# The projections' stores whose data ScalarE makes, moved from SyncE's DMA queue to ScalarE's

## The chip, the core and the metric

The kernel runs on one core of a Trainium2 chip. A core has TensorE (PE, matmuls into PSUM banks), VectorE (DVE), ScalarE (ACT), GpSimd (POOL) and SyncE (SP), which here only issues DMAs. Each engine works through its own instructions in order. A DMA is an instruction on the queue of the engine that issues it; the 16 DMA engines carry it out. The metric is the device time of one execution, in microseconds (us), lower is better. Before the change the median of three runs is 1646.94 us (1646.8 to 1649.85).

## What is computed

Two attentions over the same shapes (2048 positions, width 576, 32 heads of 18) stand side by side in the output. A is local: each position looks at 8 earlier positions, two apart. B is a full softmax attention. Both begin with a projection and end with another.

```python
def _A_ref(x, wqkv, wo):
    qkv = (lambda x, *d: x.transpose(*d))((x @ wqkv).reshape(B, S, 3, H, Dh), 2, 0, 3, 1, 4)
    ...
    logits = jnp.where(mask[None, None, :, :], logits, -1e9)
    attn = _softmax(logits, axis=-1)
    o = jnp.einsum("bhsw,bhswd->bhsd", attn, vg)
    return (lambda x, *d: x.transpose(*d))(o, 0, 2, 1, 3).reshape(B, S, D) @ wo

def _B_ref(x, wqkv, wo):
    ...
    scores = jnp.einsum("bhqd,bhkd->bhqk", q, k) * scale
    p = _softmax(scores, axis=-1)
    o = jnp.einsum("bhqk,bhkd->bhqd", p, v)
    return (lambda x, *d: x.transpose(*d))(o, 0, 2, 1, 3).reshape(B, S, D) @ wo

return jnp.concatenate([a, b], axis=-1)
```

## The kernel before

**Stages.** The projections of both attentions come first (0 to about 423 us), then the main stage: B's scores, exponentials and weighted sums step by step, with A's local attention on GpSimd beside it, and the output projections at the end. The change lies in the projections.

**How a projection is made.** Inputs and weights are split into a high and a low part, so that three products of the short format give the long one's accuracy. A loaded chunk (tiles `first`, `raw`, `more`) is rounded by ScalarE into the high part (`xhi`, `whi`, `ahi`; L369), and DVE or GpSimd subtracts to get the low part (`xlo`, `wlo`, `alo`; L370). The fifth, half-sized chunk goes through `xhl` and `whh` (L369, L404 to L406). TensorE multiplies the parts into a PSUM bank.

**How B's results leave** (`leave`, L456). For each third of the columns, each block of 512 positions and each of three row chunks, ScalarE copies the bank to `olo` (L461, which frees the bank), rounds that to `ohi` (L462), and GpSimd subtracts one from the other (L463). Then both go to the DRAM tensor `dqk` (L468): one store each for chunks 0 and 2 (128 rows), two each for chunk 1 (64 rows each, as its rows belong to queries and keys). That is 36 results with 48 stores of `ohi` and 48 of `olo`. `ohi` and `olo` have four buffers each, so the fifth result waits until the first one's store has landed. Later loads bring `dqk` back as the stacked operands `qs` and `ks` (L143, L144, on GpSimd's queue).

**How A's results leave** (`leave_a`, L649). ScalarE copies the bank to an `ohi` buffer (L651), and one store takes it to `da` (L652): 56 results, 56 stores.

**The first part (to about 83 us)** makes one third of B's queries and keys, then half of the values. The order of ScalarE's work is written out by hand: a list `ahead` of splits is popped between the chunks of the product, and the results of the block before leave in between (L503 to L519). So between 34 and 46 us ScalarE alternates: a result leaves, then a split of the next block's input or of the value weights (`whi` at L369), which the first value products need.

**The stream (83 to about 423 us)** (`stream`, L286) takes the products in groups of four over four steps; in each step two products run on the two halves of TensorE's rows. Four banks hold the group. Two products end with the third step and two with the fourth, and the next group takes their banks one step later. Between the matmuls stand the maxima of B's scores (`take` and `reduce`, L156 to L166): a matmul and a maximum on DVE. After each step `slot` runs what is due: loads of inputs (L363), of A's weights (L418, L423), splits, and loads on GpSimd's queue. When all maxima of a block are there, `mh` and `mt` (L104, L105) are loaded into two rows of `qs`, with eight small loads on SyncE's queue (L192). The last group has the first exponentials `e` (L235) in it.

**Queues.** `load` is `nc.sync.dma_start`: nearly all loads and stores stand on SyncE's queue, in the order of the program. Four first loads stand on ScalarE's, and the stacked operands' first loads on GpSimd's. The framework gives each DMA of SyncE's and ScalarE's queues one of eight semaphores in turn, and has it wait for the landing of the DMA that used the same semaphore before.

Of the kernel before, what the change touches and what calls it, by code (L numbers as in the profile page):

```python
# [7 lines left out]
F32 = mybir.dt.float32  # L8
# [23 lines left out]
HALO = DIL * (W - 1)  # L32
# [27 lines left out]
def two_attentions(ctx: ExitStack, tc, xa, wa, woa, xb, wb, wob, out):  # L60
# [5 lines left out]
    nc = tc.nc  # L66
    load = nc.sync.dma_start
# [19 lines left out]
    dqk = dram.tile([2, 2 * D, S], F32, name="dqk")  # L87
# [3 lines left out]
    da = dram.tile([3 * D, HALO + S], F32, name="da")  # L91
# [247 lines left out]
    with (tc.tile_pool(name="x", bufs=1, side="right") as xp,  # L339
# [104 lines left out]
        if True:  # L444
# [11 lines left out]
            def leave(i, b, c, ps):  # L456

                hi = xp.tile([128, 512], F32R, name="ohi", bufs=4)
                lo = low.tile([128, 512], F32R, name="olo", bufs=4)
                whole = lo.bitcast(F32)  # L460
                nc.scalar.activation(whole, ps, AF.Copy)  # L461
                nc.scalar.activation(hi, whole, AF.Copy)  # L462
                nc.gpsimd.tensor_sub(lo, whole, hi)  # L463
                for k, t in enumerate((hi, lo)):
                    at = 0
                    for base, c0, n in chunks[c]:
                        first = base + third * i + c0
                        load(dqk[k, first : first + n, 512 * b : 512 * b + 512], t.bitcast(F32)[at : at + n])  # L468
                        at += n


# [31 lines left out]
            for b in range(NB):  # L503
                pss = [bank() for _ in range(3)]
                for c in range(5):
                    for k, ps in enumerate(pss):
                        partly(c, ps, w0, x[b], slice(128 * k, 128 * k + 128), every)
                    for _ in range(2 if b == 0 and c < 3 else 1):
                        if ahead:
                            ahead.popleft()()  # L510
                    if c > 1 and out_of:
                        leave(*out_of.pop(0))
                out_of = [(0, b, k, ps) for k, ps in enumerate(pss)]
                if b == 2:
                    for c in range(5):
                        vw[1][1](c)
            do_all(ahead)
            for o in out_of:
                leave(*o)  # L519
# [120 lines left out]
            for k in range(2, 14):  # L640
                n = 46 if k == 2 else 36 + 4 * k
# [7 lines left out]
            def leave_a(c, b, n, ps):  # L649
                o = xp.tile([128, 512], F32, name="ohi", bufs=4)  # L650
                nc.scalar.activation(o[:n], ps, AF.Copy)  # L651
                load(da[128 * c : 128 * c + n, HALO + 512 * b : HALO + 512 * b + 512], o[:n])  # L652


            order = [t for i in (0, 8) for j in range(4) for t in (i + j, i + j + 4)]
# [11 lines left out]
            for b0 in range(0, NB, 2):  # L667
                for i, w in ((1, w1), (2, w2)):
                    for c in range(3):
                        for b in (b0, b0 + 1):  # L670
                            work_list.append(((b % 2, w, xs[b], slice(128 * c, 128 * c + 128), every),
                                              lambda ps: ps, lambda ps, i=i, b=b, c=c: leave(i, b, c, ps)))
# [3 lines left out]
            for c, b in order:  # L676
                n = min(128, 3 * D - 128 * c)
                work_list.append(((b % 2, ws[c][0], xas[b][0], slice(0, n), every),
                                  lambda ps, n=n: ps[:n], lambda ps, c=c, b=b, n=n: leave_a(c, b, n, ps)))
# [442 lines left out]
    while step < ALL:  # L1122
        n, kt = divmod(step, NT)
        g, b = divmod(n, NB)
# [46 lines left out]
```

## Time and profile before

| | |
|---|---|
| median of three runs | 1646.94 us (1646.8 to 1649.85) |
| the profiled execution | 1648.65 us, its span 1646.9 us |
| granted TensorE clock, mean | 1.0 |
| instructions | 33732 |
| DMA | 188.22 MB in 188353 packets, mean 114 GB/s |

How to read the profile: *busy* is the time in which an engine carries out an instruction; issuing a DMA is not busy. SPq and ACTq are the queues of SyncE and ScalarE: their rows give the start of an issue, its length, and the DMA. `out<-in` names the tiles, `L468` is a line of the kernel, `x2` the number of instructions in a row. In brackets behind a row stands the idle time of the engine before it and what ended it. The chain of work is followed back from the last instruction, at each step to what released it; a DMA in it is counted from its issue to its landing. Matmuls overlap, so their durations do not add up; their starts tell the pace.

The page's DMA view of the whole run, for orientation (a tenth of the busy share of the 16 DMA engines for each of 40 equal slices; the projections are the first ten):

```profile
DMA  8937955422616346157238225616525132034201
```

### The profile page before, as it was taken

What the parts mean: (1) busy time and instruction counts of PE and PEld (TensorE: products, weight loads), DVE (VectorE), ACT (ScalarE), POOL (GpSimd) and SP (SyncE); (2) the same over time, 40 slices, a digit from 0 to 9 for tenths busy, and PEclk for the clock granted to TensorE, in tenths of its full rate; (3) what the DMA queues carried; (4) which work ended last, traced back from release to release, by engine and by line L of the source; (5) the groups of instructions that cost most, each with busy time, mean ns of one, the idle gap of its engine ahead of it and who ended that gap; (6) DMA issues with size and microseconds to landing.
All of it is one profiled execution on the core that took longest, in us unless ns stands there. A gap on an engine that the chain in (4) does not pass through costs nothing.

```text
span 1646.9 us, 33732 instructions
## 1 busy us (share of the span) xinstructions
PE 1635.5 (99%) x12906; PEld 938.5 (57%) x12906; DVE 1395.2 (85%) x2386; ACT 1222.5 (74%) x2419; POOL 960.6 (58%) x800
## 2 busy tenths in 40 slices
PE   9999999999999999999999999999999999999999
PEld 7999778999433444444344344344444344344676
DVE  5199999999899989889889889899899999898533
ACT  6424432111899998998998998998998998998544
POOL 2406642210095995994994994994995997920000
PEclk9999999999999999999999999999999999999999
DMA  8937955422616346157238225616525132034201
GB/s 235 250 116 204 256 166 139 133 89 90 95 43 105 96 135 123 68 130 137 67 90 155 88 70 143 128 64 123 132 79 117 66 107 78 21 114 136 88 37 59
DMA packets 188353, 188.22 MB, mean 114 GB/s; under 512 B 118384, under 2 KB 132208, under 8 KB 186464
## 3 DMA queue, kind: packets, MB, share of 16 engines
q1 hardware_dynamic: 183328, 174.53, 40.9%
q0 software_dynamic: 4032, 10.63, 3.1%
q8 instruction: 101, 1.65, 0.4%
q10 hardware_dynamic: 832, 0.92, 0.2%
q14 instruction: 60, 0.49, 0.1%
HBM read 113.16 MB, written 88.12 MB: 122 GB/s over the span
## 4 chain that ended last, share of the span: by engine, by line
PE 93%; DMA 4%; ACT 1%; DVE 1%; POOL 0%; issue 0%; SPq 0%; ACTq 0%; POOLq 0%
PE po L700 30%; PE bank L229 25%; PE bank L322 14%; PE bank L159 13%; PE bank L1001 7%; PE bank L259 3%; DMA den<-o 1%; DMA dqk<-olo 1%; DMA dqk<-ohi 1%; DMA first<-wb 1%; DMA raw<-xa 1%; POOL xlo L370 0%; DMA raw<-xb 0%; DMA first<-xb 0%; PE bank L976 0%
## 5 line engine op out<-in xcount | busy, mean ns | idle before, releaser
L166 DVE TENSOR_REDUCE mx<-bank 128x1 f32<-128x512 f32 x2048 | 1286.9, 683 | 145.1 <-PE bank L159 113.7
L235 ACT ACTIVATE e<-bank 128x512 f32<-128x512 f32 x2048 | 1060.2, 613 | 95.0 <-PE bank L229 57.4
L159 PE MATMUL bank<-ks,qs 54*128 54x512 f32 x2048 | 751.0, 423 | 2.5 <-DVE mx L166 2.4
L229 PEld LDWEIGHTS bank<-qs,ks 56*128 56x128 f32 x2048 | 330.0, 185 | 450.2 <-ACT e L235 424.6
L229 PE MATMUL bank<-qs,ks 56*128 56x512 f32 x2048 | 581.5, 425 | 0.0
L700 PE MATMUL po<-e,v 128*19 128x512 f32 x4096 | 539.6, 599 | 0.0
L159 PEld LDWEIGHTS bank<-ks,qs 54*128 54x128 f32 x2048 | 340.6, 184 | 15.8 <-DVE mx L166 8.8
L832 POOL TENSOR_TENSOR pr<-aq,akv 128x1024 f32<-128x1024 f32 x72 | 158.4, 2200 | 28.3 <-DMA akv<-dpart 25.8
L700 PEld LDWEIGHTS po<-e,v 128*19 128x19 f32 x4096 | 69.5, 96 | 179.7 <-issue 169.3
L875 POOL TENSOR_TENSOR pr<-lg,akv 128x1024 f32<-128x1024 f32 x72 | 158.1, 2196 | 0.6
L836 POOL TENSOR_TENSOR pr<-pr 128x1024 f32<-128x1024 f32 x64 | 152.4, 2381 | 5.0
L651 ACT ACTIVATE ohi<-bank 128x512 f32<-128x512 f32 (+1 forms) x56 | 30.5, 595 | 147.3 <-issue 115.7
L322 PE MATMUL bank<-xhi,ahi 64*128 64x512 f32 (+1 forms) x448 | 113.7, 387 | 0.0
L322 PE MATMUL bank<-xhi,alo 64*128 64x512 f32 (+1 forms) x448 | 112.2, 388 | 0.0
L322 PE MATMUL bank<-xlo,ahi 64*128 64x512 f32 (+1 forms) x448 | 110.9, 389 | 0.4 <-POOL xlo L370 0.3
L876 POOL TENSOR_TENSOR pr<-pr 128x512 f32<-128x512 f32 x72 | 92.3, 1282 | 5.6
L370 POOL TENSOR_TENSOR alo<-raw,ahi 128x512 fp32r<-128x512 f32 (+1 forms) x14 | 17.6, 1254 | 120.6 <-ACT ahi L369 86.5
L463 POOL TENSOR_TENSOR olo<-olo,ohi 128x512 fp32r<-128x512 f32 x36 | 46.2, 1295 | 68.3 <-ACT ohi L462 60.8
L322 PEld LDWEIGHTS bank<-xhi,ahi 64*128 64x128 f32 (+1 forms) x448 | 64.6, 181 | 3.7
L322 PEld LDWEIGHTS bank<-xhi,alo 64*128 64x128 f32 (+1 forms) x448 | 63.3, 182 | 3.6
L322 PEld LDWEIGHTS bank<-xlo,ahi 64*128 64x128 f32 (+1 forms) x448 | 62.0, 182 | 5.2 <-POOL xlo L370 1.6
L1001 PE MATMUL bank<-wohi,at 64*128 64x288 f32 x512 | 64.5, 297 | 0.0
(196 smaller groups left out, 1738.5 us busy)
## 6 DMA issues: line engine op xcount, KB each, us to landing
do<-n SPq DMA_DIRECT2D x28, 512.0 KB
da<-ohi SPq DMA_DIRECT2D x52, 256.0 KB
dpart<-da SPq DMA_DIRECT2D x16, 702.0 KB
akv<-dpart SPq DMA_DIRECT2D x16, 702.0 KB
out<-y SPq DMA_DIRECT2D x32, 288.0 KB
qs<-dqk SPq DMA_DIRECT2D x30, 288.0 KB
ks<-dqk SPq DMA_DIRECT2D x30, 288.0 KB
at<-dao SPq DMA_DIRECT2D x64, 128.0 KB
```

The costliest lines, as they stand in the source:

```text
L159: nc.tensor.matmul(ps, qs[at, b, p, 128 * t : 128 * t + 128], ks[at, p, 512 * k : 512 * k + 512], start=True, stop=True)
L166: nc.vector.tensor_reduce(mx[:, r, p, t, k : k + 1], ps, axis=AX.X, op=ALU.max)
L229: nc.tensor.matmul(ps, ks[at, p, 128 * kt : 128 * kt + 128], qs[at, b, p], start=True, stop=True)
L235: nc.scalar.activation(e, ps, AF.Exp, scale=SCALE)
L259: nc.tensor.matmul(ps, a, b, start=c == i == 0, stop=c == 4 and i == 1)
L322: nc.tensor.matmul(ps, a, b, start=start, stop=stop)
L700: nc.tensor.matmul(po[32 * i : 32 * i + 19], vs[g][:, kt, 19 * i : 19 * i + 19], es[i], start=kt == 0, stop=kt == NT - 1)
L832: nc.gpsimd.tensor_mul(pr, ap(st["q"][:, 2 * c], (SUB, 2), (0, W), (1, SUB)), window(st["k"], c))
L836: nc.gpsimd.tensor_add(st["pr"], st["pr"], pr)
L875: nc.gpsimd.tensor_mul(at, ap(st["lg"], (0, 2), (SUB, W), (1, SUB)), window(st["v"], c))
L876: nc.gpsimd.tensor_add(at[:, :, :4], at[:, :, :4], at[:, :, 4:])
L1001: nc.tensor.matmul(ps, a, b, start=start, stop=stop)
```

## The change

The stores of `ohi` to `dqk` and to `da`, whose data ScalarE has just made, are issued by ScalarE's queue. The stores of `olo`, whose data GpSimd makes, stay on SyncE's. Data, shapes, buffers and the number of DMAs are as before.

```diff
                 nc.scalar.activation(hi, whole, AF.Copy)
                 nc.gpsimd.tensor_sub(lo, whole, hi)
-                for k, t in enumerate((hi, lo)):
+
+                for k, (t, store) in enumerate(((hi, nc.scalar.dma_start), (lo, load))):
                     at = 0
                     for base, c0, n in chunks[c]:
                         first = base + third * i + c0
-                        load(dqk[k, first : first + n, 512 * b : 512 * b + 512], t.bitcast(F32)[at : at + n])
+                        store(dqk[k, first : first + n, 512 * b : 512 * b + 512], t.bitcast(F32)[at : at + n])
                         at += n
...
             def leave_a(c, b, n, ps):
                 o = xp.tile([128, 512], F32, name="ohi", bufs=4)
                 nc.scalar.activation(o[:n], ps, AF.Copy)
-                load(da[128 * c : 128 * c + n, HALO + 512 * b : HALO + 512 * b + 512], o[:n])
+                nc.scalar.dma_start(da[128 * c : 128 * c + n, HALO + 512 * b : HALO + 512 * b + 512], o[:n])
```

## The prediction

> **What bounds the kernel now.** I read the page first, then its chain of work, then busy time by stretch.
>
> ```profile
> PE 1635.5 (99%) x12906; PEld 938.5 (57%) x12906; DVE 1395.2 (85%) x2386; ACT 1222.5 (74%) x2419; POOL 960.6 (58%) x800
> ...
> PE 93%; DMA 4%; ACT 1%; DVE 1%; POOL 0%; issue 0%; SPq 0%; ACTq 0%; POOLq 0%
> ```
>
> ```profile
> core 0: us, PE busy (x) PEld busy (x) DVE busy (x) ACT busy (x) POOL busy (x), PEclk, DMA share, GB/s
> 120.00:160.00 40.00, 40.00 (x349) 39.93 (x347) 39.19 (x66) 14.36 (x27) 21.55 (x23) 1.00 0.74 200
> 160.00:230.00 70.00, 67.23 (x570) 55.64 (x568) 63.73 (x104) 32.20 (x57) 49.21 (x47) 1.00 0.89 243
> 230.00:420.00 190.00, 190.00 (x1659) 177.37 (x1657) 183.01 (x303) 38.59 (x78) 29.32 (x44) 1.00 0.37 107
> 420.00:520.00 100.00, 99.90 (x698) 39.74 (x698) 90.58 (x154) 95.76 (x188) 54.09 (x43) 1.00 0.50 90
> ```
>
> TensorE sets the pace of the projections (0 to about 423 us): only 160 to 230 shows it idle, 2.8 us. Matmuls run in a fixed order and DVE is nearly full beside them, so a stall of TensorE is not caught up later; it moves the end by its own length. From 420 on ScalarE is 96% busy with exponentials, so a late start of these counts too. TensorE's waits in the projections' stream, with SyncE's issues and ScalarE's instructions by tile, are:
>
> ```profile
> PEld bank L322 <- ACT olo L461: 3.7, 3, 1.8
> PEld bank L322 <- POOL xlo L370: 1.6, 3, 0.7
> ```
>
> ```profile
> L651 ACT ACTIVATE ohi<-bank x56: 578/594/600, 219.9 to 421.9; 128x512 f32<-128x512 f32 x52, 64x512 f32<-64x512 f32 x4
> L652 SPq DMA_DIRECT2D da<-ohi x56: 319/325/1432, 221.3 to 422.5; - x56
> L468 SPq DMA_DIRECT2D dqk<-ohi x48: 319/534/1483, 29.9 to 220.3; - x48
> L462 ACT ACTIVATE ohi<-olo x36: 630/632/634, 20.1 to 210.0; 128x512 fp32r<-128x512 f32 x36
> ```
>
> The first fence gives total us, times, longest; the second min/median/max ns. So 5.3 us of waits (3.7 + 1.6) are all that a better order of stores can give back in the stream.
>
> **The change.** 104 issues (48 of dqk<-ohi, 56 of da<-ohi) leave SyncE's queue for ScalarE's. No byte and no arithmetic changes. Each store waits there for the activation just before it, then takes 0.32 to 0.53 us by the rows above. The built program adds a second wait: every DMA of SyncE and ScalarE together takes one of eight semaphores in turn, and waits until the DMA that used it last, eight before it in the program, has landed. Before, SyncE alone sat in those waits. Now ScalarE does, with its next evacuation of a PSUM bank and its next split of inputs (the xhi, whi activations) behind it, and TensorE behind those. Three rows in a row of ScalarE's, from the changed program (its lines stand one lower than before's):
>
> ```
> 61 L469 DMACopy dqk<-ohi 64x512 [waits DMAHW6_49,Activation_49]
> 62 L469 DMACopy dqk<-ohi 64x512 [waits DMAHW0_49]
> 63 L369 Activation whi<-first 128x288
> ```
>
> **Start, 34 to 47 us.** ScalarE, then DVE's last weight split, TensorE's unbroken chain, and SyncE's loads:
>
> ```profile
> 34.77 0.60 ACT L461 ACTIVATE olo<-bank 128x512 f32<-128x512 f32 x1 [6.18 <-DMA dqk<-olo]
> 36.82 0.60 ACT L461 ACTIVATE olo<-bank 128x512 f32<-128x512 f32 x1 [0.27 <-DMA dqk<-olo]
> 43.02 0.43 ACT L369 ACTIVATE whi<-first 128x288 fp32r<-128x288 f32 x1
> 45.17 0.43 ACT L369 ACTIVATE whh<-first 128x288 fp32r<-128x288 f32 x1
> ```
>
> ```profile
> 46.63 0.44 DVE L370 TENSOR_TENSOR wll<-first,whh 128x288 fp32r<-128x288 f32 x1
> ```
>
> ```profile
> 38.06 44.48 PE bank L259 x312
> ```
>
> ```profile
> 30.69 1.41 SPq L468 DMA_DIRECT2D dqk<-olo  x1
> 41.14 3.51 SPq L363 DMA_DIRECT2D raw<-wb  x6
> ```
>
> From 34.77 to 45.17 ScalarE has only one gap, 0.27 us. Five results leave in it; seven stores now stand between them (two results have two each): 7 x 0.534 = 3.7 us. The weights' last split ends at 47.07. TensorE needs it after 33 matmuls of 512 columns and 13 of 288; at the chain's rate (44.48 us for 33 x 512 and 279 x 288 columns, 0.457 ns each) that is 9.4 us after 38.06, at 47.5, so 0.4 us is spare. Sum **+3.3 us**. Lower bound +1.2: 0.32 us an issue (2.2 in all), less the spare 0.4, less 0.6 because the store that frees olo goes a place earlier (30.69 was the second store on SyncE). Upper bound +5: three of the stores share semaphores with raw<-wb loads, whose issues end at 44.65; with the 4 us from issue to landing that SyncE's first olo store took (30.69 to 34.77) ScalarE would stand until 48.7, and its last three splits, now done at 45.60, would end near 50.3. I take the median issue, and no such wait, since SyncE with half the stores reaches those loads sooner.
>
> **Stream, 155 to 230 us.** A step of the stream is 3.7 us (155.60 to 159.31 below), and a bank is due one step after its product ends.
>
> ```profile
> 155.60 0.60 ACT L461 ACTIVATE olo<-bank 128x512 f32<-128x512 f32 x1 [8.44 <-issue]
> 159.31 0.60 ACT L461 ACTIVATE olo<-bank 128x512 f32<-128x512 f32 x1 [1.30 <-PE bank L322]
> 160.47 0.58 ACT L461 ACTIVATE olo<-bank 128x512 f32<-128x512 f32 x1
> 172.80 0.63 ACT L369 ACTIVATE xhi<-raw 128x512 fp32r<-128x512 f32 x1 [9.45 <-DMA raw<-xa]
> 204.54 0.60 ACT L461 ACTIVATE olo<-bank 128x512 f32<-128x512 f32 x1 [3.68 <-PE bank L322]
> ```
>
> ```profile
> 157.30 1.88 SPq L192 DMA_DIRECT2D qs<-mt  x2
> 159.22 0.40 SPq L363 DMA_DIRECT2D raw<-xa  x1
> ...
> 207.98 1.61 SPq L363 DMA_DIRECT2D raw<-xa  x3
> 209.69 3.11 SPq L363 DMA_DIRECT2D more<-xa  x6
> ```
>
> ```profile
> 174.82 8.36 DMA raw<-xa
> 183.19 3.63 DMA dqk<-ohi
> ```
>
> The results of 155.60 have four stores (64 rows each). Their semaphores were last used by the small mh and mt loads; the last mt is issued until 159.18, so the fourth store leaves at about 160.2. The first store of 159.31's pair waits for an olo store, eight earlier, that SyncE issues behind the mt and xa loads, at about 160.8; with 3.6 us of flight (the last fence: issue to landing) it goes at 164.4. The last evacuation, now 160.47, ends at about 165.4, due 163.0: **+2.4**. The same happens at 204.54: the four stores share semaphores with xa loads now issued from 207.98 on. SyncE, rid of sixteen hi issues since 160 (8.5 us at 0.534), should reach them some 5 us sooner (my choice between 0 and 8.5): first store at 207, second result out at 209.6, due 206.8: **+2.8**, and **+0.8** on the next step. At 220 the da stores follow mh loads that the new program puts ahead of them; half of that delay shows: **+0.8**. Against this stand the two waits above: SyncE's xa loads and olo stores go earlier, so the xhi of 172.80 and the banks behind it come in time. I take both as gone, **-5.3**. Net **+1.5 us**. Bounds: nothing added, all removed, -5.3; all added, none removed, +6.8. No row shows ScalarE waiting on such a semaphore, so both ends stay.
>
> **Rest of A, 230 to 416 us: 0.** A pair of evacuations ends 1.1 us after its step and would end 0.5 us later with a store of 0.33 us between; 3.7 us are allowed. In this stretch the loads whose semaphores the stores inherit were issued well before (DMA share 0.37). If one is late, over 2 us would have to pass before TensorE felt it.
>
> **Handover, 416 to 425 us.**
>
> ```profile
> 416.34 1.07 ACT L651 ACTIVATE ohi<-bank 64x512 f32<-64x512 f32 x2 [10.46 <-issue]
> 417.31 2.04 ACT L235 ACTIVATE e<-bank 128x512 f32<-128x512 f32 x4
> 421.36 1.07 ACT L651 ACTIVATE ohi<-bank 64x512 f32<-64x512 f32 x2 [2.01 <-issue]
> 422.33 2.04 ACT L235 ACTIVATE e<-bank 128x512 f32<-128x512 f32 x4
> ```
>
> Each pair of evacuations becomes 2 x (0.594 + 0.325) = 1.84 us long ahead of the exponentials, instead of 0.97 (416.34 to 417.31): 0.9 us. The second delay counts in full, since ScalarE is the busy engine from there; of the first, TensorE hides half: **+1.3** (0.7 to 1.9). The copies to dpart move ahead in SyncE's queue; nothing in the chain waits for them.
>
> **Sum:** 3.3 + 1.5 + 1.3 = +6.1 us on the profiled execution's 1648.65 (its span 1646.9 and 1.75 around it): 1654.8. That execution lies 1.7 above the median of the runs shown, 1646.94, so the forecast against the median is **1653.0 us**.
>
> **Rivals.** *Hidden* (within 3.3 us of 1646.94): only SyncE's issue time changes place, eight semaphores notwithstanding; the start costs 1.2, the handover 0.7, the stream gives back 2: 0, so 1646.9. For it: SyncE's own issue is nowhere in the chain (SPq 0%); against it: ScalarE's gapless start. [...]
>
> *Faster*: TensorE's waits of 160 to 230 are there because loads of xa stand behind stores on one queue. If the loads overtake and ScalarE's waits are short, the stream gives 5.3, the start takes 1.2 and the handover 0.7: -3.4, 1643.5. It decides if the olo and xa landings come at least 5 us sooner than now at 160. The DMA share of 0.89 there speaks against it. [...]
>
> *Worse*: the saturated DMA keeps SyncE as late as now (207.98), the second stall becomes 7 us instead of 2.8, and the start takes 5: 6.1 + 4.2 + 1.7 = +12, about 1659. It decides if SyncE's row for those xa loads stays at its distance of 3.4 us behind the result of 204.54.
>
> That the change would not do what it says is excluded: the built program has the stores on ScalarE's queue.
>
> **How the numbers follow.** A measurement tells about 0.2% (3.3 us) from no change. Forecast 0.60 (1650.3 to 1658), hidden 0.19, faster 0.09, worse 0.12. So slower 0.72, same 0.19, faster 0.09. The range 1644.5 to 1660 leaves out most of *faster* and the end of *worse*.
>
> **What would show it.** ScalarE's queue should hold DMA rows between L462 and the next activation, with ScalarE's waits put down to DMA landings of wb, mt and xa; whi of 43.02 at about 46; TensorE waiting some 3 us in the first value product, again near 165 and 207 for olo; no 9.45 us before the xhi of 172.80; steps of 3.7 us unchanged after 230. It is wrong if TensorE shows no wait before 60, or if a stall appears after 230.

## The result and the profile after

The changed kernel takes 1666.24 us (median of four runs, 1665.06 to 1670.06) against 1647.55 of the kernel before beside it: a ratio of 1.0109 with a 95% interval of 1.0094 to 1.0124, that is +18.7 us. The forecast was 1653.0 (+6.1), its range 1644.5 to 1660. A second set of runs gave 1.0132 (1.0103 to 1.0160). The profiled execution has a span of 1665.5 us, 18.6 more than the one before.

The page's first line and its chain, where TensorE's and ScalarE's busy time are up by 8.7 and 6.6 us and DVE's is down:

```profile
PE 1644.2 (99%) x12906; PEld 941.0 (57%) x12906; DVE 1389.7 (83%) x2386; ACT 1229.1 (74%) x2419; POOL 960.7 (58%) x800
...
PE 92%; DMA 3%; ACT 1%; issue 0%; POOL 0%; DVE 0%; ACTq 0%; SPq 0%; POOLq 0%
```

ACTq has 0% of the chain, though the issues on that queue are the cause: an engine that stands in a semaphore's wait is not busy, and its queue's row starts only when the wait is over (the row of 188.19 below starts 2.6 us after its data were ready). The page does not show this loss. It is found by matching the two traces, instruction by instruction. The tables below give how much later the same maximum (the k-th TENSOR_REDUCE on DVE) starts than in the first trace of before; in that trace the first six of them start at 83.9, 150.4, 202.6, 245.6, 414.5 and 450.6 us, and the seventh, near the end, at 1538.5.

| lateness in us at the maximum of | 83.9 | 150.4 | 202.6 | 245.6 | 414.5 | 450.6 | 1538.5 |
|---|---|---|---|---|---|---|---|
| the changed kernel | 5.68 | 6.24 | 10.92 | 17.39 | 17.46 | 19.11 | 18.56 |

So the loss is: start +5.7, stream +11.7, rest of A +0.1, handover +1.7, main stage -0.5. Within the stream the lateness rises by 2.6 between 159 and 164 us of before's time, by 5.4 at 180 and by 5.9 between 208 and 212; and it falls by 1.1 at 176 to 179 and by 2.2 at 191 to 197. (The rest, about 1.1, comes in steps of 0.6 us or less at 137 and from 212 on.)

TensorE's waits for ScalarE and GpSimd from 83 to 250 us, which answer to the 3.7 and 1.6 us that the prediction took from before's stream (total, times, longest):

```profile
PEld bank L322 <- ACT olo L461: 10.3, 4, 4.0
...
PEld bank L322 <- POOL xlo L370: 1.2, 1, 1.2
```

ScalarE's rows of the start. They answer to 34.77, 43.02 and 45.17 in the prediction:

```profile
35.61 0.60 ACT L461 ACTIVATE olo<-bank 128x512 f32<-128x512 f32 x1 [5.31 <-DMA dqk<-olo]
...
47.24 0.45 ACT L369 ACTIVATE whi<-first 128x288 fp32r<-128x288 f32 x1 [1.19 <-DMA raw<-wb]
...
49.98 0.43 ACT L369 ACTIVATE whh<-first 128x288 fp32r<-128x288 f32 x1
```

TensorE at that place:

```profile
49.79 0.40 PE L259 MATMUL bank<-whi,xhi 128*128 128x288 f32 x1 [1.16 <-ACT whi L369]
...
50.61 0.55 PE L259 MATMUL bank<-wlo,xhi 128*128 128x288 f32 x1 [0.29 <-DVE wlo L370]
```

The bracket behind 47.24 names a load of wb, but ScalarE did not stand for it. The issues of the two stores before that split fill the gap: they run from 46.08, when their data were ready, to 47.19. In the kernel that has only the start of the change (*e1* below) the same gap is put down to the issue. The first row is the changed kernel's, the second *e1*'s:

```profile
46.08 1.11 ACTq L469 DMA_DIRECT2D dqk<-ohi  x2
```

```profile
46.21 0.45 ACT L369 ACTIVATE whi<-first 128x288 fp32r<-128x288 f32 x1 [1.19 <-issue]
```

Between 35.61 and 50.41 the seven issues leave gaps of 1.18, 0.40, 0.40, 1.19 and 0.40 us, 3.6 us in all, and every store starts as soon as its data are ready. So in the start no store waits for a landing. The last split ends at 50.41, 4.81 us later than before; 0.8 of that is there already at the copy of 35.61.

ScalarE's rows of the stream: copies of a bank (L461), and its own DMA issues (ACTq, L469) between them; the roundings between (L462, 0.63 us each) are left out:

```profile
161.84 0.60 ACT L461 ACTIVATE olo<-bank 128x512 f32<-128x512 f32 x1 [7.36 <-issue]
163.57 2.60 ACTq L469 DMA_DIRECT2D dqk<-ohi  x2
166.26 0.60 ACT L461 ACTIVATE olo<-bank 128x512 f32<-128x512 f32 x1 [3.16 <-DMA dqk<-ohi]
...
184.28 0.60 ACT L461 ACTIVATE olo<-bank 128x512 f32<-128x512 f32 x1
188.19 1.69 ACTq L469 DMA_DIRECT2D dqk<-ohi  x2
189.99 0.60 ACT L461 ACTIVATE olo<-bank 128x512 f32<-128x512 f32 x1 [4.39 <-DMA raw<-xa]
...
215.46 0.60 ACT L461 ACTIVATE olo<-bank 128x512 f32<-128x512 f32 x1 [7.24 <-PE bank L322]
218.46 2.89 ACTq L469 DMA_DIRECT2D dqk<-ohi  x2
221.47 0.60 ACT L461 ACTIVATE olo<-bank 128x512 f32<-128x512 f32 x1 [4.75 <-DMA more<-xa]
224.02 1.28 ACTq L469 DMA_DIRECT2D dqk<-ohi  x2
225.40 0.60 ACT L461 ACTIVATE olo<-bank 128x512 f32<-128x512 f32 x1 [2.67 <-DMA more<-xa]
```

Each time one bank is copied out, two stores follow that must wait, and the second bank, long finished, is copied out 4.4, 5.7 and 6.0 us after the first (before: 1.2, as 159.31 and 160.47 in the prediction show). SyncE's queue at the last two places:

```profile
175.68 4.68 SPq L363 DMA_DIRECT2D raw<-xa  x4
...
214.99 1.61 SPq L363 DMA_DIRECT2D raw<-xa  x3
216.70 3.16 SPq L363 DMA_DIRECT2D more<-xa  x6
```

The loads of 175.68 were issued by 180.36. ScalarE's store of 188.19 needs the third of them to have landed, eight DMAs back in the program; the store's data were ready at 185.6. At the first place the two stores need loads of mh that SyncE issued at 156.73 and 159.34, and that landed 6.8 and 6.4 us later; by the trace's semaphore records the stores' rows start 0.08 and 0.02 us after these landings (163.49 and 165.69). In this trace the 960 DMAs of the two queues use eight semaphores, 120 each.

And now the clock. Stretches of the changed kernel (columns: TensorE's busy time and matmuls, weight loads, DVE, ScalarE, GpSimd, then the granted clock, the DMA share and GB/s):

```profile
core 0: us, PE busy (x) PEld busy (x) DVE busy (x) ACT busy (x) POOL busy (x), PEclk, DMA share, GB/s
...
50.70:54.10 3.40, 3.40 (x15) 3.40 (x16) 0.59 (x2) 2.04 (x4) 1.96 (x2) 0.50 0.52 190
54.10:57.50 3.40, 3.40 (x27) 3.40 (x27) 0.40 (x1) 2.46 (x8) 2.10 (x4) 1.00 0.94 221
...
190.70:194.10 3.40, 3.40 (x16) 2.74 (x18) 1.38 (x2) 1.08 (x2) 1.27 (x1) 0.51 0.81 228
194.10:197.50 3.40, 3.40 (x32) 3.10 (x32) 3.15 (x5) 3.00 (x6) 3.12 (x4) 1.00 0.78 177
...
221.40:228.20 6.80, 6.08 (x28) 4.84 (x30) 3.12 (x6) 3.50 (x6) 2.56 (x2) 0.50 0.86 276
228.20:231.60 3.40, 3.40 (x32) 2.94 (x30) 3.22 (x7) 2.97 (x7) 3.09 (x3) 1.00 0.77 234
```

Three of the four stalls are followed by a stretch of 3.4 or 6.8 us in which TensorE gets half its clock: 14 to 16 matmuls in 3.4 us, where it does 27 to 32 at full clock. TensorE is "busy" there, so no view of waits shows it. At full clock the same work would take half of the busy time, so the estimate of this loss is (3.40 + 3.40 + 6.08) / 2 = **6.4 us, a third of the whole**. In the stream it fits: from 83 to 250 us TensorE's idle time rises from 3.3 to 10.1 us, and these 6.7 us and the 4.7 of clock make 11.4 of the 11.7.

The handover, as predicted: each pair of copies now has two issues in it, of 0.45 us each, where the prediction took 0.325.

```profile
440.05 0.59 ACT L652 ACTIVATE ohi<-bank 64x512 f32<-64x512 f32 x1 [1.96 <-PE bank L322]
440.67 0.45 ACTq L653 DMA_DIRECT2D da<-ohi  x1
441.17 0.59 ACT L652 ACTIVATE ohi<-bank 64x512 f32<-64x512 f32 x1 [0.53 <-ACT ohi L652]
441.79 0.45 ACTq L653 DMA_DIRECT2D da<-ohi  x1
```

### The profile page after: what moved, and what is told of

Its sections match the earlier page's. It is cut to its first block, busy times and chain, and to the rows that moved or that the text cites. A ratio compares the mean times of both kernels' runs of the same rounds, so it can differ in the third digit from the quotient of the medians.

```text
span 1665.5 us, 33697 instructions
## 1 busy us (share of the span) xinstructions
PE 1644.2 (99%) x12906; PEld 941.0 (57%) x12906; DVE 1389.7 (83%) x2386; ACT 1229.1 (74%) x2419; POOL 960.7 (58%) x800
## 3 DMA queue, kind: packets, MB, share of 16 engines
q8 instruction: 101, 1.65, 0.4%
## 4 chain that ended last, share of the span: by engine, by line
PE 92%; DMA 3%; ACT 1%; issue 0%; POOL 0%; DVE 0%; ACTq 0%; SPq 0%; POOLq 0%
PE po L701 30%; PE bank L229 25%; PE bank L322 15%; PE bank L159 13%; PE bank L1002 7%; PE bank L259 2%; DMA raw<-xa 1%; DMA den<-o 1%; PE bank L977 0%; DMA more<-xa 0%; DMA dqk<-olo 0%; POOL xlo L370 0%; ACT olo L461 0%; DMA raw<-wb 0%; ACT ohi L652 0%
## 5 line engine op out<-in xcount | busy, mean ns | idle before, releaser
L461 ACT ACTIVATE olo<-bank 128x512 f32<-128x512 f32 x36 | 21.3, 593 | 67.3 <-PE bank L322 25.8
L104 POOL CAST mh<-mt 128x32 fp32r<-128x32 f32 x32 | 6.8, 212 | 101.4 <-DVE mt L180 101.2
```

## The experiments

**Theory A**: ScalarE stands in waits for the landing of the DMA that used the same semaphore, eight before in the program, and TensorE's clock is halved after the stalls. **Theory B**: ScalarE only pays the time of the issues. Both can hold, at different places. **Theories C to E** are named where they are used. All kernels in one table; the ratio is to runs of before on the same chip, the columns are lateness as above.

| kernel | ratio (95%) | 83.9 | 150.4 | 202.6 | 245.6 | 414.5 | 450.6 | 1538.5 |
|---|---|---|---|---|---|---|---|---|
| changed kernel | 1.0109 (1.0094 to 1.0124) | 5.68 | 6.24 | 10.92 | 17.39 | 17.46 | 19.11 | 18.56 |
| a2_after_again | 1.0132 (1.0103 to 1.0160) | 5.86 | 6.81 | 10.31 | 18.41 | 18.50 | 20.12 | 28.77 |
| e0_before_again | one execution | -0.94 | -0.93 | -2.81 | -2.03 | -2.05 | -2.06 | -1.14 |
| e14_before_again | one execution | -0.95 | -0.93 | -2.24 | -1.47 | -1.48 | -1.53 | 0.24 |
| e1_start_only | 1.0044 (1.0031 to 1.0057) | 4.64 | 4.65 | 4.28 | 6.96 | 6.94 | 6.89 | 10.06 |
| e2_stream_only | 1.0064 (1.0048 to 1.0081) | -0.30 | 0.24 | 3.95 | 8.62 | 8.59 | 8.61 | 11.70 |
| e3_da_only | 1.0047 (1.0031 to 1.0063) | -0.84 | -0.80 | -0.55 | 4.90 | 4.97 | 6.69 | 9.81 |
| e7_idle_copies | 1.0049 (1.0030 to 1.0068) | 0.93 | 1.15 | 0.46 | 5.96 | 8.33 | 8.99 | 12.02 |
| e4_pairs_only | 1.0054 (1.0034 to 1.0075) | -0.68 | -0.08 | 5.17 | 5.80 | 5.78 | 5.80 | 8.35 |
| e5_singles_only | 1.0065 (1.0047 to 1.0083) | -0.77 | -0.74 | 6.92 | 11.40 | 11.37 | 11.40 | 10.78 |
| e9_both_then_store | 1.0091 (1.0067 to 1.0116) | -0.67 | 1.79 | 3.32 | 14.20 | 14.18 | 14.25 | 22.80 |
| e6_pool_hi | 1.0022 (1.0004 to 1.0039) | -1.02 | 1.20 | 1.42 | 2.89 | 2.87 | 2.83 | 5.71 |
| e12_xa_pool | 1.0068 (1.0044 to 1.0093) | 3.69 | 4.12 | 3.68 | 5.32 | 6.76 | 8.51 | 15.30 |
| e15_loads_pool | 1.0066 (1.0046 to 1.0087) | 4.84 | 5.29 | 10.30 | 11.89 | 11.95 | 15.09 | 18.40 |
| e10_one_store | 1.0489 (1.0459 to 1.0519) | | | | | | | |
| e11_one_store_act | 1.0543 (1.0504 to 1.0581) | | | | | | | |
| e13_before_xa_pool | 0.9986 (0.9971 to 1.0000) | -0.43 | -0.41 | -3.42 | -4.17 | -4.16 | -4.24 | -1.42 |
| e17_before_xa_pool_5 | 0.9978 (0.9966 to 0.9990) | -0.67 | -0.66 | -2.98 | -3.71 | -3.73 | -3.74 | -2.10 |
| e16_xa_lo_pool | 1.0130 (1.0112 to 1.0147) | -0.25 | 3.39 | 4.21 | 15.66 | 15.64 | 15.66 | 19.91 |

Two things to read first. The two later traces of **before itself** are 0.9 us earlier at the start than the first one, and lack its wait of 1.4 us at 195; so a lateness of -1 to -2 means "as before", and against them the changed kernel's start costs 6.6 us. And from 450.6 to 1538.5 most single executions gain or lose some us at one place near 910 us (on TensorE, a maximum comes late there in before too: 1.71 us of waiting in its first trace, with a clock of 1.00 behind it): that is why the last column is no measure of a part, and the columns up to 450.6 are.

```profile
909.61 0.18 PEld L159 LDWEIGHTS bank<-ks,qs 54*128 54x128 f32 x1 [2.02 <-DVE mx L166]
```

This row is of before's first trace; before's own runs beside the experiments went from 1644.9 to 1657.4 us.

### The parts alone

```diff
-store = nc.scalar.dma_start                          # every hi store
+store = nc.scalar.dma_start if i == 0 else load      # e1; leave_a on load
+store = nc.scalar.dma_start if i > 0 else load       # e2; leave_a on load
+store = load                                         # e3; leave_a on nc.scalar
```

> Only the stores of the first third (the start, up to 83 us) are issued by ScalarE; all others stay with SyncE. Theory A (ScalarE stands in waits for the landing of the DMA that used the same semaphore, and TensorE's clock is halved after the stall): the first maximum comes 5.7 us later than before, as in the changed kernel, and the rest adds nothing: +5 to +6.5, about 1653. Theory B (ScalarE only pays the issue time, 0.33 to 0.6 us a store, as the prediction had it): +3.3 us and no half clock. Theory C (the loss of the start is made up later, because DVE and the loads have slack): within 2 us of before.

> Only the stores of the second and third thirds (the stream, 125 to 230 us) are issued by ScalarE. Theory A: no delay at 83 us, then three stalls of TensorE, each at a result with two stores, with about the changed kernel's sizes (2.6, 5.1 and 6.0 us, less some 3 us won back in between): +10 to +13 in all, about 1659. Theory B: the pairs of results get 0.33 to 0.6 us longer each, which the step of 3.7 us hides: within 2 us of before. If the stream's stalls were a consequence of the late start (another phase against the loads), they would be missing or much smaller here.

> Only the 56 stores of the second attention's results (from 220 us on) are issued by ScalarE. Theories A and B agree: nothing up to 416 us but at most 0.5 us at 220, then 1.3 to 1.9 us at the handover to the exponentials: +1.5 to +2.2, about 1649. A loss above 4 us would mean that the loads whose semaphores these stores inherit are late in this stage too, against the prediction's zero.

*e1*: 5.6 us at the first maximum against the later traces of before (4.64 + 0.94), with a granted clock of 0.57 between 49 and 53 us, and no part is made up later (C falls). Each theory has one half here. The issues alone make ScalarE late, as in theory B (its gap of 1.19 us is shown above); TensorE is 3.0 us late when the half clock begins, and 1.6 more after it. That the rest adds nothing did not come true: 2.7 us more come between 202.6 and 245.6. *e2*: three stalls with no late start ahead of them, 8.9 us from 83.9 to 450.6 (-0.30 to 8.61): the stream's stalls are its own. *e3*: the handover is as expected, 4.97 to 6.69 = 1.72, and nothing happens between 245.6 and 414.5 (0.07). But 5.5 us come at 222, which I had put at 0.5: the first store of `da` waits there for loads of mh that the new program puts ahead of it, as ScalarE's row in e3 says:

```profile
225.27 0.35 ACTq L653 DMA_DIRECT2D da<-ohi  x1
225.74 0.60 ACT L652 ACTIVATE ohi<-bank 128x512 f32<-128x512 f32 x1 [6.12 <-DMA qs<-mh]
```

In the whole change this stall is missing, because the one of 209 us stands in front of it. So the parts do not add up: 7.3 + 10.6 + 7.8 = 25.7 us by their ratios to 1650.39, against 18.7 and (a2) 21.8 for the whole.

### ScalarE's time without the waits

```diff
+for _ in chunks[c]:                                   # in leave, stores on SyncE as before
+    nc.scalar.activation(spent[:, :w], hi.bitcast(F32)[:, :w], AF.Copy)    # w = 128, or 288 twice
+nc.scalar.activation(spent[:n, :128], o[:n, :128], AF.Copy)                # in leave_a
```

> All stores are issued by SyncE as before, but ScalarE does a small copy (128 columns for a result with one store, 288 columns for each of two, about 0.30 and 0.43 us) at each place where the change puts a store. This is ScalarE's time without the waits. Theory A: the start loses 2 to 4 us, the stream under 1, the handover 0.8 to 1.5: +3 to +6 in all, 1650 to 1653. Theory B: nearly the changed kernel's +18.7 us.

The start costs 1.9 us (0.93 + 0.94) instead of 5.6, with a granted clock of 1.00 from 45 to 57.5 us. But the copies are shorter than the issues that they stand for: from the first copy of a bank to the last split ScalarE needs 2.6 us more than before, and 4.0 more in the change. So the difference is longer issues and the clock, not waits for landings. The total, +8 us, is more than theory A expected. 5.5 us of it come in one place, at 223, where ScalarE in e7 waits for a buffer of `ohi`, that is for a store on SyncE behind the loads of xa:

```profile
221.99 0.63 ACT L406 ACTIVATE ohi<-raw 64x512 fp32r<-64x512 f32 x1 [6.60 <-DMA dqk<-ohi]
...
227.22 0.60 ACT L655 ACTIVATE ohi<-bank 128x512 f32<-128x512 f32 x1 [3.04 <-DMA dqk<-ohi]
```

Before has the same wait (e14: 6.1 us, once), of which TensorE feels under 1 us. Another 2.4 us are spread evenly over the rest of A (5.96 to 8.33), where the changed kernel's issues cost nothing (0.07); how the idle copies cost them stays open. So this kernel takes too little at the start and too much after it, and is no clean measure of theory B.

### Which stores stall

```diff
+store = nc.scalar.dma_start if i > 0 and c == 1 else load     # e4, results with two stores
+store = nc.scalar.dma_start if i > 0 and c != 1 else load     # e5, results with one store
```

> The kernel before, unchanged, for a trace of it from the chip on which the three runs beside it are made. Theory A: TensorE waits 1 to 4 us in all between 170 and 230 us here too, and some 2 us at about 910 us, at places where the first trace shows ScalarE waiting for a buffer of ohi or TensorE for a maximum; these places are before's own and no part of the change. If it shows none of the waits at 175, 223 and 915 us that the single-part kernels showed, these belong to the parts.

> In the stream alone, and there only the results with two stores (the chunk of 64 + 64 rows), the stores of ohi are issued by ScalarE. In the built program all but the first four of these take semaphores last used by loads of mh, mt or xa. Theory A: all three stalls are here, so about the loss of the kernel with the stream alone: +8 to +12. Theory B (issue time): 16 issues of some 0.5 us, hidden by the steps: within 2 us of before. Theory D (the loss comes from the number of stores that left SyncE): a half of the stream's loss.

> In the stream alone, and there only the results with one store (128 rows), the stores of ohi are issued by ScalarE. Their semaphores were mostly last used by stores of olo or by loads some 8 us older. Theory A: no stall at 160, 180 and 209 us; within 2.5 us of before. Theory B: the same. Theory D: a half of the stream's loss, some +5.

*e0* (1647.5) has a wait of TensorE of 1.1 us at 173 and one of 1.9 at 908, which are before's own, and loses 0.8 us between 202.6 and 245.6: what e1, e3 and e7 lose there beyond that (2.7, 5.5 and 5.5 us in all) is not before's own. *e4* has its loss in one stall at 180 (4.6 us idle, and a granted clock of 0.65 from 187.2 to 190.7); those at 160 and 209, which theory A expected too, are 1.0 and 1.3 us. *e5* should have lost nothing by theory A as I had put it, and lost most: stalls at 162, 199 and 219. I had looked only for loads among the semaphores' last users. ScalarE in e5:

```profile
165.60 0.33 ACTq L469 DMA_DIRECT2D dqk<-ohi  x1
166.05 0.60 ACT L461 ACTIVATE olo<-bank 128x512 f32<-128x512 f32 x1 [6.22 <-DMA dqk<-ohi]
```

and SyncE in e5 a little earlier:

```profile
159.20 2.31 SPq L469 DMA_DIRECT2D dqk<-ohi  x2
161.60 1.18 SPq L469 DMA_DIRECT2D dqk<-olo  x2
```

The store of ScalarE whose data were ready at 159.8 needs the first `olo` store of 161.60 to have landed. SyncE itself had been standing in such waits (on the loads of mh and mt before it), so that store was late, and ScalarE inherited SyncE's lateness plus a flight of 4.0 us (161.60 to 165.60). Theory A is thereby wider than I had it: **here a DMA of ScalarE's starts only after the landing of the one that used its semaphore last, eight before it in the program, whatever that one carries** (eight stores of the change, between 163 and 225 us, start 0.02 to 0.08 us after it). Not the kind of the DMA eight before decided (loads of mh in the change, a store of olo in e5), but how far the other queue had come.

### Copy out both banks, then store

```diff
+store = lambda *a: held.append(a)          # hi, i > 0
+if i and b % 2 == 0:                       # the second result of a step
+    while held:
+        nc.scalar.dma_start(*held.pop(0))
```

> In the stream alone, ScalarE first copies out both banks of a step and only then issues the stores of both results; the stores wait for the same kind of semaphores (mh, mt, xa). Theory A: the second bank no longer stands behind the first result's store; the stall at 180 us (5.1) is gone, since nothing else is due there, and those at 160 and 209 us shrink to what the next step's banks feel: +1 to +6. Theory B or D: as the kernel with the stream alone, +10.

A miss, and by far (+15 us): the stall at 180 is gone, as expected, but the one at 160 grows to 4.7 us, and at 215 ScalarE stands for 12 us, and TensorE for 8.9:

```profile
216.24 6.17 ACTq L475 DMA_DIRECT2D dqk<-ohi  x4
222.51 0.60 ACT L463 ACTIVATE olo<-bank 128x512 f32<-128x512 f32 x1 [12.23 <-DMA dqk<-ohi]
```

Four stores in a row have four such waits in a row, and now the next step's two banks are behind all of them. Putting the waiting instruction later changed here only which work is behind it.

### Other queues for the stores, or for the loads

```diff
+store = nc.gpsimd.dma_start                            # e6: hi stores and da stores
+xas[b][1](c, nc.gpsimd.dma_start)                      # e12: the changed kernel, loads of xa
+(nc.gpsimd.dma_start if projecting else load)(...)     # e15: as e12, and the loads of mh and mt
```

DMAs of GpSimd's queue have semaphores of their own: in the traces of before and of the changed kernel its 36 DMAs use another eight than the 960 of SyncE and ScalarE, and in e6's built program its 140 do.

> All 104 stores of the change are issued by GpSimd's queue instead of ScalarE's. DMAs of that queue have semaphores of their own, so no store waits for a DMA of SyncE's and ScalarE waits for none; SyncE is rid of the same 104 issues as in the changed kernel. Theory A (the loss is ScalarE standing in the shared semaphores' waits): the start, the three stalls of 160 to 222 us and the handover are gone; GpSimd pays 0.6 to 0.9 us an issue: between 3 us faster and 6 slower than before. Theory E (the loss comes from the stores leaving SyncE's order, by which loads and stores meet differently at the DMA engines): about the changed kernel's loss, +15 or more.

> The changed kernel with one more edit: the loads of xa are issued by GpSimd's queue, so that they have semaphores of their own and no store of ScalarE's can stand behind one. The stores of ohi stay with ScalarE. Theory A: the start stays (+4.5 to 5.7), the stall at 160 us stays (its stores take semaphores of mh and mt), those at 180 and 209 us shrink to 1 or 2 us: +6 to +12 in all. Theory B or E: as the changed kernel, +16 to +19.

> The changed kernel, with the loads of xa and those of mh and mt in the projections issued by GpSimd's queue: in the stream the stores of ScalarE then share semaphores with earlier stores only. Theory A: the stall at 160 us goes too; what is left is the start (4.5 to 5.7) and the handover (1.4 to 1.9): +5 to +9 against before, if GpSimd has the time for some 100 more issues of 0.6 us. Theory E (new places among the DMAs): the stall at 160 us stays, +10 or more.

*e6* takes the same 104 issues from SyncE as the change does, and gives them to an engine that shares no semaphore: +3.6 us (1.0022) instead of 18.7, nothing at the start (-1.02, as before), nothing at the handover (2.87 to 2.83). Theory E, that the stores' new place among the DMAs makes the loss, falls for some four fifths of it (e6's interval is 0.7 to 6.4 us). But e6 spares ScalarE the issues too, and does not tell them from the waits. *e12* does: it leaves the stores with ScalarE and takes only the loads of xa off the shared semaphores. The start and the 160 us stall stay, those at 180 and 209 shrink to 0.7 and 1.0 us. Up to 245.6 us its lateness is 5.32 instead of 17.39. Its granted clock is 1.00 in each of the stretches shown above for the change, and half of the difference (6.4 of 12.1 us) is the clock that the change loses. Its result with two stores, which cost 5.4 us in the change, in e12 (L462 left out again):

```profile
181.73 0.60 ACT L461 ACTIVATE olo<-bank 128x512 f32<-128x512 f32 x1
183.07 1.12 ACTq L469 DMA_DIRECT2D dqk<-ohi  x2
184.29 0.60 ACT L461 ACTIVATE olo<-bank 128x512 f32<-128x512 f32 x1 [1.25 <-PE bank L159]
```

*e15* takes mh and mt off too. The stalls at 160 and 209 shrink to 1.4 and 0.8 us, as theory A has it, but a new one of 5 us stands at 180: ScalarE waits there for the loads of xa themselves, the first of which is issued by GpSimd at 170.6 and lands 8.5 us later. Why so late was not tried.

```profile
ACT xhi L369 <- DMA raw<-xa: 6.9, 1, 6.9
```

The handover costs 3.1 us there, twice what was expected. So e15's total (+10.9, expected 5 to 9) does not confirm theory A; the stalls at 160 and 209 do.

### One store instead of two

```diff
-for base, c0, n in chunks[c]:                          # e10 on before, e11 on the change
-    store(dqk[k, first : first + n, ...], t.bitcast(F32)[at : at + n])
+store(rows(dqk[k, base + third * i + c0, 512 * b], ((D - 128) * S, m), (S, n), (1, 512)), t.bitcast(F32))
```

> The kernel before, with one DMA instead of two for the results whose rows belong to queries and keys: 24 DMAs fewer (72 instead of 96 to dqk), all on SyncE, same bytes. Eight semaphores then reach further back in time. Theory A: the waits that before itself has for buffers of ohi (5.2 us of ScalarE at 218 us) shrink: 1 to 4 us faster than before. If the DMA engines set those waits: no change.

> The changed kernel, with one DMA instead of two for the results whose rows belong to queries and keys, on ScalarE for ohi and on SyncE for olo: 24 DMAs fewer. Theory A: ScalarE's stores reach further back, to DMAs that landed earlier; the start loses two issues (-1), the stalls shrink by a third to a half: +8 to +14 against before. Theory B: -1 to -2 against the changed kernel.

They are 81 and 89 us slower than before, nearly all of it in the projections; both expectations were wrong. ScalarE in e10 waits up to 10 us for such a store to land:

```profile
43.79 0.60 ACT L461 ACTIVATE olo<-bank 128x512 f32<-128x512 f32 x1 [10.00 <-DMA dqk<-olo]
```

while the 16 DMA engines are busy for less than half of the time. The same stretch in e10, and after it in e14 (before):

```profile
28.00:60.00 32.00, 21.05 (x84) 16.28 (x82) 8.28 (x9) 11.21 (x22) 6.40 (x5) 0.85 0.43 138
```

```profile
28.00:60.00 32.00, 32.00 (x192) 29.13 (x191) 13.08 (x16) 19.10 (x47) 17.45 (x20) 1.00 0.91 256
```

The share is 0.43 in e10 against 0.91 before. Why one store in place of two does this was not shown: no other shape of it was tried, and no view here shows which of the engines worked. The kernels say nothing on theory A.

### A version faster than both

```diff
+xas[b][1](c, nc.gpsimd.dma_start)                      # e13, e17: the kernel before, loads of xa
+store = nc.gpsimd.dma_start if i else load             # e16: as e13, and the stores of olo
```

> The kernel before, with the loads of xa on GpSimd's queue; all stores stay with SyncE. Theory A: SyncE no longer stands behind these loads' landings, so the stores that free ohi land earlier, and ScalarE's wait of 5.2 us before the ohi at 218 us shrinks: between 3 us faster and 1 slower than before. Theory E: no change.

> The kernel before once more, on the chip of these runs: 1646 to 1655, with 1 to 3 us of waits of TensorE between 170 and 230 us.

> The changed kernel once more, on the chip of these runs: +15 to +20 us against before, with the same places of loss (start 5.7, stream 10 to 13, handover 1.4).

> The kernel before with the loads of xa on GpSimd's queue, in more rounds: 1 to 3 us faster than before, with no wait of TensorE over 1 us between 170 and 230 us; no change if the first result was chance.

> As the other, and in the stream the stores of olo are issued by GpSimd, which makes the data: SyncE keeps the stores of ohi, ScalarE issues none. No engine that TensorE waits for stands in a shared semaphore's wait. Up to 4 us faster than before if GpSimd (70 percent busy from 160 to 230 us) hides 32 more issues of 0.6 us; up to 6 slower if it does not, by late xlo.

Without the change, the loads of xa on GpSimd's queue make the kernel faster by 0.22% (0.10 to 0.34%), some 3.6 us: 1647.92 against 1652.04. The gain is where theory A puts it, between 150 and 246 us (-0.66 to -3.71, before's own later traces -0.93 to -1.47 and -2.03). TensorE's wait for ScalarE's copies from 83 to 230 us is 1.1 us in e17 and 2.1 in e14. *a2* repeats the change's places (start 6.8 against e14 beside it, stream 12.6, handover 1.6). *e16* shows the other end, far outside what was expected (+21 us, where 6 was the worst): 32 more issues on GpSimd, and its own `xlo` comes late, with 8.8 us of TensorE's waiting at once:

```profile
PEld bank L322 <- POOL xlo L370: 9.2, 1, 9.2
```

## Why the prediction was wrong

The sign was right, the size was not: +6.1 forecast, +18.7 measured, outside the range. By its own steps:

- **Start, +3.3 (1.2 to 5): measured +5.7** (6.6 against the later traces of before). The mechanism was right, and so was the size of what it named: the seven issues take 3.6 us of ScalarE (forecast 3.7), without a wait for wb, as assumed, and TensorE is 4.1 us late when its clock falls, 0.4 of it from before the first moved store. What failed is a term that the sum had at nothing: half a clock for 3.4 us, which adds 1.6. (The upper bound is mis-added too: splits that end at 50.3 make +4.3, not +5.)
- **Stream, net +1.5 (-5.3 to +6.8): measured +11.7.** This step failed, in three ways.
  - *What is added.* The stall at 163 to 165 was put at +2.4 and is 2.6, but that is luck: the prediction lets the stores of 155.60's results go in time and has the next pair's first store wait for an olo store, while it was the first pair's stores that waited, for loads of mh with 6.8 and 6.4 us of flight. The one at 204 to 212 was put at 2.8 + 0.8 and is 5.9, but 3.0 of that is clock, so the wait itself was put a little too high; SyncE did come nearly as much sooner as I had chosen (its xa loads start 0.5 us before the result of 215.46, in before 3.4 behind that of 204.54; 3.9 us, where I took 5), and the loads that the two stores waited for took 2.9 and 4.2 us to land, where I used 3.6. The one at 180 was not in the sum at all: 5.4 us, 1.7 of it clock. It could have been: the prediction quotes the row "174.82 8.36 DMA raw<-xa", a load of xa that takes 8.4 us to land, and it quotes it for its other line. With 8.4 instead of 3.6 a store of the result that leaves its bank at 176.93 waits until 183.2. I had used the flight of a store for that of a load, in the stage where the DMA share is 0.89. The +0.8 at 220 did not show as such: after 212 the lateness rises by 0.6 in all.
  - *What is removed.* The 5.3 us of before's waits were counted as the change's gain. They are waits of weight loads, which overlap matmuls, and the prediction's own table has TensorE idle for only 2.8 us from 160 to 230. The lateness does fall, by 1.1 us at 176 to 179 and by 2.2 at 191 to 197, but the 2.2 us are in e2, e3 and e7 and in both later traces of before as well: that wait belonged to one execution. So against the first trace 1.1 us are the change's gain. A wait of a single trace is no gain until it is known to come back.
  - *The clock.* 1.7 + 3.0 us of the stream's loss is half clock after the stalls.
- **Rest of A, 0: measured +0.07.** Right: all steps keep their pace. The hint that a late load would have to be over 2 us late to be felt was not tested here, since the stream's stall hides the one of e3.
- **Handover, +1.3 (0.7 to 1.9): measured +1.65**, 1.72 in e3. Right in kind and within its bounds.
- **The rivals.** *Worse* named the place and the price (+12) but from another cause, SyncE staying late; SyncE did not. *Hidden* had only SyncE's issue time change place. e6 is close to that (+3.6 us for 104 issues moved), and the change is not (+18.7), because ScalarE's queue shares its eight semaphores with SyncE's, and because ScalarE has no gap at the start into which its issues would fit (0.27 us in all from 34.77 to 45.17). *Faster*, in which the loads of xa overtake the stores, is what e13 and e17 are nearest to (0.22% in e17), but with the loads on the queue that has semaphores of its own.

Of the signs of being wrong neither came: TensorE waits before 60, and no stall appears after 230. Of the signs of being right most came: ScalarE's waits put down to xa, TensorE's waits near 165 and 207, no long wait before that xhi (none over 2.0 us is put down to a load of xa). Three did not: the wait put down to wb is issue time, none is put down to mt, and TensorE waits 1.2 and 0.3 us in the first value product, not some 3. So the waits that the prediction named came, for the most part. It failed in the stream's sum, which left out the stall at 180 (5.4 us) and took back 5.3 us where 1.1 came, and in having no term for the clock (6.4 us).

What stays open: why the loads of 178.8 and 180.0 took some 9 us to land in the changed kernel, and by how much the half clock changes what later loads meet. Neither was tried by itself. Nor were the 2.7 us (0.8 of them before's own) that e1 loses after 202.6, far from its stores.

## What to carry to other kernels

Before moving a DMA to a second queue, ask which semaphore it takes and who used it last. Here two queues share eight: ScalarE's store of 163.57 started 0.08 us after the landing of SyncE's load eight before it, and the engine that copies out PSUM banks paid for the other's lateness (second banks 4.4 to 6.0 us after the first, 1.2 before). Price such a wait with the flight of that very DMA in that stage (8.4 us for a load of xa, where the store's was 3.6). Try the DMA on a queue with semaphores of its own (+3.6 us in e6 against +18.7; but +21 in e16), or leave it with the engine that has nothing behind it. A bracket behind a row names the last semaphore that came, not always what the engine stood for (47.24, a load of wb): look whether issues fill the gap. Where the engine had no gap, its issue time counted in full (seven issues, 3.6 us at the start). And give every stall of TensorE a second price: what the clock does after it (here an estimated 6.4 us of 18.7).

## What the runs showed of the hardware

**Half of TensorE's clock after a short stall.** 1.16 us of waiting at 48.6 to 49.8 us was followed by 3.4 us at half clock in the changed kernel (0.50 from 50.7 to 54.1). In e12 TensorE waits equally long at the same instruction (1.17 us, then a start at 49.26), and keeps its clock:

```profile
45.00:49.00 4.00, 3.10 (x15) 2.22 (x13) 0.60 (x2) 2.30 (x5) 1.85 (x2) 1.00 0.99 319
49.00:53.00 4.00, 3.45 (x23) 3.18 (x24) 1.52 (x3) 3.22 (x7) 2.10 (x3) 1.00 0.63 213
```

So the length of a wait alone does not tell what follows; what does was not shown. TensorE's other waits of more than 1.1 us in the changed kernel's trace end at 166.91 (1.44 us), 190.63 (3.54), 222.12 (3.00), 436.68 (1.25) and 928.22 (1.24). With those of 3.54 and 3.00 us came half clock, from 190.7 for 3.4 us and from 221.4 for 6.8; after the three others the clock is 1.00. In the first trace of before it is 1.00 after both such waits, 1.38 us up to 196.54 and 1.71 up to 909.61. At the second of these places the weight load waits 2.0 us in that trace (909.61, shown above), and 2.2 and 2.0 us in the two later ones. The mean granted clock of the later two is 0.999, that of the first 1.000; where in them it was lower was not shown. Of before's own runs beside the experiments the fastest, 1644.9 us, has a granted clock of 1.0 and the slowest, 1657.4, one of 0.997.
